# Column-tiled transposes, and bias sums moved later, at the head of a six-layer cross network on one core

## The chip, the cores and the metric

The kernel runs on one core of one Trainium2 chip. A core has TensorE (PE, matrix products; its weight loads are listed apart as PEld), VectorE (DVE), ScalarE (ACT), GpSimd (POOL), SyncE (SP, here only a queue of DMA issues) and 16 DMA engines. The metric is device time in microseconds of one execution; the median of several runs is compared. The profile is of one execution, with its own time.

## The reference, cut to what matters

```python
B, F, D, L = 4096, 26, 16, 6
Din = min(F * D, 1024)          # 416
# x0 [4096, 416], ws [6, 416, 416], bs [6, 416], all bf16
def reference(x0, ws, bs):
    x = x0
    for l in range(ws.shape[0]):
        x = x0 * (x @ ws[l] + bs[l]) + x
    return x
```

Each layer adds x0 times something to x, so x after layer l is x0 times (1 + the sum over the layers so far of x @ ws + bs). [...]

## The kernel before, in words

**Layout.** The work is done transposed, features on partitions and batch rows along the free axis. The 416 features are three chunks of 128 (c or k or m = 0, 1, 2) and a tail of 32. The 4,096 rows are four stripes of 1,024 (s), each in two halves of 512. The 32 tail features would fill only 32 partitions, so four groups of 256 rows lie side by side on 128 partitions (x0t_sb, xt_sb).

**One layer of one stripe on TensorE** (lines 318 to 431). First the *main steps* of half 0: for each of three input chunks k and three output chunks m, four matmuls of 128x32 weights side by side (`tile_mm`, L265; the tile position is a group of 32 columns of the array) over 512 rows. Then the *row matmuls* (L393, L409), which take the tail features with 32x128 weights: part 0 and part 1. Then the *tail matmuls* (L423 to L428, recorded at L265 with 256 columns), which compute the tail outputs. Then the main steps of half 1. VectorE turns each PSUM bank into the next layer's chunk (L537), ScalarE and GpSimd do the same for the tail (L595, L242, L566). Every engine follows its program in order, and semaphores (`s_...`) join them: `wait_ge(s, n)` holds the engine until s reaches n.

**The head, layer 0 of stripe 0.** Its input must first be turned. Blocks of 128x128 of x0 are loaded in natural layout into xin_sb: rows 0 to 255 (first part, h = 0, s_xin[0]), 256 to 511 (second part, h = 1), 512 to 767 (third part). The last 256 rows of the stripe come by a transposing DMA (L158), which SyncE issues once the first part has landed (L157).

- SyncE issues at L134 to L136: the biases into bsa_sb, xin_sb's first part, its third part. ScalarE issues at L137 to L139 the second part, layer 0's weights (w_sb), the tail features of the last rows (xtl_sb). VectorE clears wc_sb and sets row 0 of bsa_sb to one (L141, L142; s_zero). GpSimd makes the identity and the triangle u_sb (L211, L215; s_set) and issues small weight loads.
- TensorE runs 40 *filler* matmuls on constants (L129 to L133), then `bias_sums` (L295: 16 matmuls with 7 rows; u_sb makes running sums), one more group of four fillers (L270, L306), then the transposes of the first two parts (L308 to L316): for each of six blocks two 128x128 transposes into bf16 PSUM.
- The order of the six blocks is written out: `IN_ORDER = ((1, 0), (1, 1), (1, 2), (0, 0), (0, 1), (0, 2))`, pairs (h, c). VectorE copies blocks with c other than 1 to x0T_sb (L512, s_inD), ScalarE those with c = 1 (L562, s_inA). VectorE first copies the bias sums to cb_sb (L506, s_cb).
- Layer 0's main steps run k by k (L357): k = 0 waits for three VectorE copies (L349), k = 1 for two ScalarE copies, k = 2 for four VectorE copies. After the first of the three steps of k = 2, TensorE does the `tail_inputs` (L275: sixteen 128x32 matmuls with the identity, signal s_tp, copied by ScalarE at L576 to x0t_sb, s_te) and the `third_input` (L284: the third part, 24 matmuls with the identity into fp32 PSUM, copied at L517 and L578). Then the last two main steps.
- Row matmuls part 0 wait for x0t_sb (s_te) and five VectorE copies; part 1 for the sixth and ScalarE's third copy (L400 to L403). The tail matmuls wait for the transposing DMA (L422).

Of the kernel before, what the change touches and what calls it, by code (L numbers as in the profile page):

```python
# [11 lines left out]
def bass_standalone__dcn_v2_cross__recsys_kernel(  # L12
# [6 lines left out]
    B, D = x0.shape  # L19
# [13 lines left out]
    with ExitStack() as es:  # L33
# [22 lines left out]
        ones_sb = sb("ones_sb", [128, 256])  # L56
        bsa_sb = sb("bsa_sb", [L + 1, D])
        u_sb = sb("u_sb", [L + 1, L])
        cb_sb = sb("cb_sb", [128, NC + 1, L], FP32)
# [38 lines left out]
        IN_BANKS = ((3, 4, 6), (0, 5, 7))  # L98
        IN_ORDER = ((1, 0), (1, 1), (1, 2), (0, 0), (0, 1), (0, 2))
        THIRD = (3, 6, 7)  # L100
# [27 lines left out]

        for q in range(4 * 10):  # L129
            nc.tensor.matmul(  # L130
                ps[lane(q % 4), 7, 0:256], lhsT=CONST[:, 0:32], rhs=CONST, start=True, stop=True,
                skip_group_check=True, tile_position=(0, 32 * (q % 4)),
            )  # L133
        nc.sync.dma_start(bsa_sb[1:L + 1, :], bs[:, :]).then_inc(s_bs, 16)  # L134
        nc.sync.dma_start(xin_sb[:, 0:2, :], x0_w[:, 0, :, :]).then_inc(s_xin[0], 16)
        nc.sync.dma_start(xin_sb[:, 4:6, :], x0_w[:, 2, :, :]).then_inc(s_xin[2], 16)  # L136
        nc.scalar.dma_start(xin_sb[:, 2:4, :], x0_w[:, 1, :, :]).then_inc(s_xin[1], 16)  # L137
        nc.scalar.dma_start(w_sb[:, 0, :, :], wmain(0)).then_inc(s_w[0], 16)
        nc.scalar.dma_start(xtl_sb[:, :, :], x0_v[:, 6:JS, DF:D]).then_inc(s_xtl0, 16)  # L139
        nc.gpsimd.memset(ones_sb[:, :], 1.0).then_inc(s_ones, 1)  # L140
        nc.vector.memset(wc_sb[:, :, :], 0.0).then_inc(s_zero, 1)  # L141
        nc.vector.memset(bsa_sb[0:1, :], 1.0).then_inc(s_zero, 1)  # L142

# [59 lines left out]
        def _(pool):  # L203
            def load_wc(i, g):
# [10 lines left out]
            pool.affine_select(  # L215
                out=u_sb[:, :], in_=ones_sb[0:L + 1, 0:L], pattern=[[1, L]],
                compare_op=ALU.is_ge, fill=0.0, base=1, channel_multiplier=-1,
            ).then_inc(s_set, 1)
            for g in (0, 2):
                load_wt(pool, g, 0, 1, s_wtp)  # L220
            pool.wait_ge(s_zero, 1)
            for i in range(2):
# [3 lines left out]
            for s in range(NS):  # L226
                pool.wait_ge(s_te, s + 1)
                for l in range(L):
                    n = s * L + l + 1
                    if n == NL:  # L230
                        break
                    if n == 1:
                        pool.tensor_scalar(
                            out=cq_sb[:, 0:NC + 1], in0=cb_sb[:, :, L - 1], scalar1=-1.0, scalar2=None, op0=ALU.add
                        ).then_inc(s_cq, 1)
                        pool.wait_ge(s_cq, 1)
                        pool.tensor_tensor(
                            out=cq_sb[:, NC + 1:NC + 2], in0=cq_sb[:, NC:NC + 1], in1=cb_sb[:, NC, L - 2:L - 1], op=ALU.subtract
                        ).then_inc(s_cq, 1)
# [23 lines left out]
        def _(pe):  # L263
# [5 lines left out]

            def fill(n):  # L270
                for i in range(n):
                    for q in range(4):
                        tile_mm(ps[lane(q), 7, 0:256], CONST[:, 0:32], CONST, q, True)

# [9 lines left out]
            def third_input():  # L284
                pe.wait_ge(s_inD, 4)
                for c in range(NC):
                    for j in range(2):
                        for q in range(4):
                            f0 = c * 128 + 32 * q
                            ins = tile_mm(  # L290
                                ps[lane(q), THIRD[c], j * 128:j * 128 + 128], xin_sb[:, 4 + j, f0:f0 + 32], ident[:, :], q, True
                            )
                    ins.then_inc(s_inT, 1)

            def bias_sums():  # L295
                pe.wait_ge(s_bs, 16)
                pe.wait_ge(s_zero, 2)
                pe.wait_ge(s_set, 2)
                for c in range(NC + 1):
                    for q in range(4):  # L300
                        f0 = c * 128 + 32 * q if c < NC else DF
                        ins = tile_mm(ps[lane(q), 1, c * 8:c * 8 + L], bsa_sb[:, f0:f0 + 32], u_sb[:, :], q, True)
                ins.then_inc(s_cbp, 1)

            bias_sums()
            fill(1)  # L306
            pe.wait_ge(s_set, 1)
            for i, (h, c) in enumerate(IN_ORDER):  # L308
                if c == 0:
                    pe.wait_ge(s_xin[h], 16)  # L310
                for j in range(2 * h, 2 * h + 2):
                    ins = pe.transpose(  # L312
                        out=psT[:, IN_BANKS[h][c], (j % 2) * 128:(j % 2 + 1) * 128],
                        in_=xin_sb[:, j, c * 128:(c + 1) * 128], identity=ident[:, :],
                    )
                ins.then_inc(s_inT, 1)  # L316

            for s in range(NS):
                for l in range(L):
# [27 lines left out]
                    def before_a(k):  # L347
                        if n == 0:
                            pe.wait_ge((s_inD, s_inA, s_inD)[k], (3, 2, 4)[k])  # L349
                        else:  # L350
                            pe.wait_ge(s_xa, NC * (n - 1) + k + 1)
                            if l == 0 and k == 0:
                                pe.wait_ge(s_x0T[s], 16)

                    if n == 0:
                        pe.wait_ge(s_w[0], 16)
                        for k in range(NC):  # L357
                            before_a(k)
                            for m in range(NC):
                                if k == 0 and m == 1:  # L360
                                    pe.wait_ge(s_cb, 1)
                                if k == 2 and m == 1:
                                    pe.wait_ge(s_xin[2], 16)
# [35 lines left out]
                    for part in range(2):  # L399
                        if n == 0 and part == 1:  # L400
                            pe.wait_ge(s_inD, 6)
                            pe.wait_ge(s_inA, 3)
                            pe.wait_ge(s_wc[0], 32)  # L403
# [100 lines left out]
        def _(dve):  # L504
            dve.wait_ge(s_cbp, 1)
            dve.tensor_copy(  # L506
                out=cb_sb[:, :, :], in_=ps[:, 1, 0:8 * (NC + 1)].rearrange("p (c e) -> p c e", e=8)[:, :, 0:L],
            ).then_inc(s_cb, 1)
            for i, (h, c) in enumerate(IN_ORDER):
                if c != 1:  # L510
                    dve.wait_ge(s_inT, i + 1)
                    dve.tensor_copy(  # L512
                        out=x0T_sb[:, c, h * 256:(h + 1) * 256], in_=psT[:, IN_BANKS[h][c], 0:256]
                    ).then_inc(s_inD, 1)
            for c in (0, 2):
                dve.wait_ge(s_inT, 2 * NC + c + 1)
                dve.tensor_copy(out=x0T_sb[:, c, 512:768], in_=ps[:, THIRD[c], 0:G]).then_inc(s_inD, 1)  # L517
            dve.wait_ge(s_cb, 1)
# [37 lines left out]
        def _(act):  # L556
# [20 lines left out]
            act.wait_ge(s_inT, 2 * NC + 2)  # L577
            act.activation(out=x0T_sb[:, 1, 512:768], in_=ps[:, THIRD[1], 0:G], func=ACTF.Copy).then_inc(s_inA, 1)  # L578
            act.wait_ge(s_cb, 1)
# [79 lines left out]
```

## Time and profile before

| what | value |
|---|---|
| median of 7 runs | 128.24 us |
| all runs | 128.09, 128.13, 128.18, 128.24, 128.72, 129.0, 130.84 us |
| the profiled execution's own time | 128.19 us |
| its span in the profile | 127.0 us |
| TensorE busy | 123.4 us (97%), 2,410 matmuls |
| VectorE, ScalarE, GpSimd busy | 99.9, 67.6, 24.1 us |
| first filler starts / first transpose / first main step | 0.83 / 3.62 / 5.13 us |
| first row matmul / first tail matmul of layer 0 | 7.92 / 8.53 us |
| one layer of one stripe on TensorE | 4.87 us |
| loads of xin_sb, from issue to landing (least, median, most) | 2.5, 2.6, 3.7 us |

Times inside a profile count from the start of its span; the 1.2 us between span and time lie around it. A row of the timeline gives start, length, engine, line, operation, output and input tile, partitions x elements and the count of merged instructions; in brackets stands the idle time ahead of the first and what ended it. A matmul's length is that of one pass through the array, and matmuls overlap, so pace is read from the distance between starts. A waiting instruction is put down to the releaser that came last by the profile.

### The profile page before, as it was taken

What the parts mean: (1) busy time and instruction counts of PE and PEld (TensorE: products, weight loads), DVE (VectorE), ACT (ScalarE), POOL (GpSimd) and SP (SyncE); (2) the same over time, 40 slices, a digit from 0 to 9 for tenths busy, and PEclk for the clock granted to TensorE, in tenths of its full rate; (3) what the DMA queues carried; (4) which work ended last, traced back from release to release, by engine and by line L of the source; (5) the groups of instructions that cost most, each with busy time, mean ns of one, the idle gap of its engine ahead of it and who ended that gap; (6) DMA issues with size and microseconds to landing.
All of it is one profiled execution on the core that took longest, in us unless ns stands there. A gap on an engine that the chain in (4) does not pass through costs nothing.

```text
span 127.0 us, 5323 instructions
## 1 busy us (share of the span) xinstructions
PE 123.4 (97%) x2410; PEld 62.4 (49%) x2410; DVE 99.9 (79%) x154; ACT 67.6 (53%) x146; POOL 24.1 (19%) x44
## 2 busy tenths in 40 slices
PE   7999999999999999999999999999999999999991
PEld 5654545445445445445445445445444444454660
DVE  2449779779779779789788797797797797797973
ACT  0637357377726455575744563574762574566830
POOL 7512202202102013022022023022021021220550
PEclk9999999999999999999999999999999999999999
DMA  4952599600009879620007969970006910430006
GB/s 113 272 130 31 148 256 190 185 0 5 0 3 137 144 109 237 220 71 5 0 5 139 102 129 245 295 241 0 5 0 48 207 24 0 168 106 5 0 29 244
DMA packets 31889, 13.49 MB, mean 106 GB/s; under 512 B 24950, under 2 KB 31868, under 8 KB 31868
## 3 DMA queue, kind: packets, MB, share of 16 engines
q1 hardware_dynamic: 30476, 12.12, 45.0%
q10 hardware_dynamic: 1200, 0.99, 2.5%
q8 instruction: 19, 0.31, 1.0%
q0 software_dynamic: 192, 0.06, 0.3%
q14 instruction: 2, 0.02, 0.0%
HBM read 3.86 MB, written 3.41 MB: 57 GB/s over the span
## 4 chain that ended last, share of the span: by engine, by line
PE 97%; DVE 0%; issue 0%
PE ps L265 82%; PE ps L393 10%; PE ps L130 2%; PE ps L449 2%; PE ps L312 1%; PE ps L464 1%; DVE o_sb L550 0%; PE ps L488 0%; PE ps L409 0%; PE ps L494 0%
## 5 line engine op out<-in xcount | busy, mean ns | idle before, releaser
L537 DVE SCALAR_TENSOR_TENSOR xT_sb<-ps,cb_sb,x0T_sb 128x512 bf16<-128x512 f32 x120 | 81.0, 744 | 16.4 <-PE ps L393 16.3
L265 PE MATMUL ps<-xT_sb,w_sb 128*32 128x512 bf16 (+1 forms) x1596 | 84.2, 364 | 0.0
L265 PEld LDWEIGHTS ps<-xT_sb,w_sb 128*32 128x32 bf16 x1596 | 40.9, 97 | 37.2 <-issue 4.0
L566 ACT ACTIVATE xt_sb<-xt_sb 32x256 bf16<-32x256 bf16 x76 | 31.5, 414 | 15.7 <-POOL xt_sb L242 15.1
L595 ACT ACTIVATE t_sb<-ps,cb_sb 64x256 f32<-64x256 f32 x46 | 21.6, 469 | 31.1 <-PE ps L265 30.8
L242 POOL TENSOR_TENSOR xt_sb<-t_sb,x0t_sb 128x256 bf16<-128x256 f32 x20 | 13.5, 673 | 81.4 <-ACT t_sb L595 81.4
L265 PE MATMUL ps<-x0T_sb,w_sb 128*32 128x512 bf16 (+1 forms) x336 | 18.6, 366 | 0.0
L537 DVE SCALAR_TENSOR_TENSOR xo_sb<-ps,cb_sb,x0T_sb 128x512 bf16<-128x512 f32 x18 | 12.1, 744 | 2.5 <-PE ps L393 2.5
L265 PEld LDWEIGHTS ps<-x0T_sb,w_sb 128*32 128x32 bf16 x336 | 8.6, 97 | 7.7 <-issue 1.3
L393 PE MATMUL ps<-xt_sb,wt_sb 32*128 32x512 bf16 x76 | 11.5, 379 | 0.0
L614 ACT ACTIVATE x0t_sb<-x_sb 32x512 bf16<-32x512 bf16 x12 | 7.5, 626 | 0.3
L409 PE MATMUL ps<-xt_sb,wt_sb 32*128 32x512 bf16 x38 | 7.4, 385 | 0.0
L393 PE MATMUL ps<-xt_sb,wc_sb 32*128 32x256 bf16 x76 | 7.3, 268 | 0.0
L393 PEld LDWEIGHTS ps<-xt_sb,wt_sb 32*128 32x128 bf16 x76 | 2.2, 92 | 8.1 <-DVE xT_sb L537 8.1
L393 PEld LDWEIGHTS ps<-xt_sb,wc_sb 32*128 32x128 bf16 x76 | 3.8, 93 | 2.2
L242 POOL TENSOR_TENSOR xot_sb<-t_sb,x0t_sb 128x256 bf16<-128x256 f32 x3 | 2.0, 674 | 12.6 <-ACT t_sb L595 12.6
L550 DVE SCALAR_TENSOR_TENSOR o_sb<-ps,x0n_sb 128x416 bf16<-128x416 f32 x6 | 3.3, 585 | 1.0 <-PE ps L494 0.9
L570 ACT ACTIVATE xo_sb<-ps,cq_sb 128x512 bf16<-128x512 f32 x5 | 3.3, 686 | 1.1 <-PE ps L393 1.1
L130 PE MATMUL ps<-const-bfloat16-1.0 128*32 128x256 bf16 x40 | 2.3, 416 | 0.8 <-PEq L644 0.8
L561 ACT ACT_TABLE_LOAD x1 | 1.3, 1283 | 3.3 <-issue 3.3
L449 PE MATMUL ps<-w_sb,xT_sb 128*128 128x416 bf16 x12 | 2.8, 340 | 0.0
L265 PE MATMUL ps<-w_sb,xT_sb 128*32 128x416 bf16 x48 | 2.6, 339 | 0.0
(52 smaller groups left out, 39.9 us busy)
## 6 DMA issues: line engine op xcount, KB each, us to landing
out_dram<-o_sb SPq DMA_DIRECT2D x2, 832.0 KB, 5.3
w_sb<-in_ws_dram SPq DMA_DIRECT2D x5, 312.0 KB, 3.9
x0n_sb<-in_x_dram SPq DMA_DIRECT2D x1, 832.0 KB, 5.4
out_dram<-o_sb SPq DMA_DIRECT2D x1, 624.0 KB, 4.1
out_dram<-o_sb SPq DMA_DIRECT2D x3, 208.0 KB, 2.0
xin_sb<-in_x_dram SPq DMA_DIRECT2D x2, 208.0 KB, 3.1
out_dram<-o_sb ACTq DMA_DIRECT2D x2, 208.0 KB, 2.0
w_sb<-in_ws_dram ACTq DMA_DIRECT2D x1, 312.0 KB, 3.5
```

The costliest lines, as they stand in the source:

```text
L130: nc.tensor.matmul(ps[lane(q % 4), 7, 0:256], lhsT=CONST[:, 0:32], rhs=CONST, start=True, stop=True, skip_group_check=True, tile_position= ...
L242: pool.tensor_tensor(out=dst, in0=t32_sb[:, n % 2, :], in1=x0t_sb[:, s, 0:G], op=ALU.mult).then_inc(s_xt, 1)
L265: return pe.matmul(dst, lhsT=lhsT, rhs=rhs, start=start, stop=True, skip_group_check=True, tile_position=(0, 32 * q),)
L393: return pe.matmul(dst, lhsT=lhsT, rhs=srct[lane(g), cols], start=l == 0 and start, stop=True, skip_group_check=True, tile_position=(32 * ...
L409: pe.matmul(ps[:, NC * h + 2, :], lhsT=wt_sb[lane(g), l, 0:128], rhs=srct[lane(g), :].rearrange("p (b r) -> p b r", b=2)[:, ::-1, :], star ...
L449: pe.matmul(ps[:, NAT_BANKS[t], 0:D], lhsT=xT_sb[:, (L - 1) % 2, k, rows], rhs=w_sb[:, L - 1, k, :], start=False, stop=True, skip_group_ch ...
L537: dve.scalar_tensor_tensor(out=dst, in0=ps[:, NC * half + c, :], scalar=cb_sb[:, c, l:l + 1], in1=x0T_sb[:, c, o:o + H], op0=ALU.add, op1= ...
L550: dve.scalar_tensor_tensor(out=o_sb[:, j0 + t, :], in0=ps[:, NAT_BANKS[t], 0:D], scalar=1.0, in1=x0n_sb[:, t, :], op0=ALU.add, op1=ALU.mul ...
L566: ins = act.activation(out=buf[lane(g), G:2 * G], in_=buf[lane(g ^ 1), 0:G], func=ACTF.Copy)
L570: act.activation(out=xo_sb[:, NS - 1, c, half * H:(half + 1) * H], in_=ps[:, NC * half + c, :], func=ACTF.Identity, bias=cq_sb[:, c:c + 1] ...
L595: ins = act.activation(out=t32_sb[HALVES[h], n % 2, :], in_=tail(h), func=ACTF.Identity, bias=cb_sb[HALVES[h], NC, l:l + 1],)
L614: ins = act.activation(out=x0t_sb[lane(g), s + 1, :].rearrange("p (b n) -> p b n", b=2), in_=src[:, ::-1, :] if g % 2 else src, func=ACTF. ...
```

## The change

Fillers, transposes, bias sums, the order of the blocks and of SyncE's first loads change; what is computed does not.

- 52 fillers instead of 40; the single filler group and the `fill` helper go. `bias_sums` leaves the front.
- The transposes of all three parts become four transposes of 32 columns each side by side (`tile_tp`), in the tile shape that fillers and main steps have. The third part's now go to bf16 PSUM as well.
- Block (0,0) is turned third instead of fourth, and k = 0 waits for two VectorE copies instead of three.
- `bias_sums` stands ahead of the first main step of k = 2, followed by `tail_inputs` and `third_input`, which so stand one main step earlier. bsa_sb and u_sb get 128 partitions (zeros below the seven rows), and the sums go to bank 4 instead of bank 1. The wait for cb_sb moves from the second main step to row matmuls part 1; GpSimd gets one of its own.
- SyncE issues the biases after the two loads of xin_sb, and waits ahead of all three for VectorE's new first memset, which clears bsa_sb.

```diff
-        bsa_sb = sb("bsa_sb", [L + 1, D])
-        u_sb = sb("u_sb", [L + 1, L])
+        bsa_sb = sb("bsa_sb", [128, D])
+        u_sb = sb("u_sb", [128, L])
...
-        IN_ORDER = ((1, 0), (1, 1), (1, 2), (0, 0), (0, 1), (0, 2))
+        IN_ORDER = ((1, 0), (1, 1), (0, 0), (1, 2), (0, 1), (0, 2))
...
-        for q in range(4 * 10):
+        for q in range(4 * 13):
...
-        nc.sync.dma_start(bsa_sb[1:L + 1, :], bs[:, :]).then_inc(s_bs, 16)
+        nc.sync.wait_ge(s_zero, 1)
         nc.sync.dma_start(xin_sb[:, 0:2, :], x0_w[:, 0, :, :]).then_inc(s_xin[0], 16)
         nc.sync.dma_start(xin_sb[:, 4:6, :], x0_w[:, 2, :, :]).then_inc(s_xin[2], 16)
+        nc.sync.dma_start(bsa_sb[1:L + 1, :], bs[:, :]).then_inc(s_bs, 16)
...
+        nc.vector.memset(bsa_sb[:, :], 0.0).then_inc(s_zero, 1)
         nc.vector.memset(wc_sb[:, :, :], 0.0).then_inc(s_zero, 1)
+        nc.vector.wait_ge(s_zero, 1)
         nc.vector.memset(bsa_sb[0:1, :], 1.0).then_inc(s_zero, 1)
...
-            pool.wait_ge(s_zero, 1)
+            pool.wait_ge(s_zero, 2)
...
                     if n == 1:
+                        pool.wait_ge(s_cb, 1)
...
+            def tile_tp(dst, src, q):
+                return pe.transpose(out=dst, in_=src, identity=ident[:, :], tile_position=(0, 32 * q))
...
-                            ins = tile_mm(
-                                ps[lane(q), THIRD[c], j * 128:j * 128 + 128], xin_sb[:, 4 + j, f0:f0 + 32], ident[:, :], q, True
+                            ins = tile_tp(
+                                psT[lane(q), THIRD[c], j * 128:j * 128 + 128], xin_sb[:, 4 + j, f0:f0 + 32], q
                             )
...
             def bias_sums():
                 pe.wait_ge(s_bs, 16)
-                pe.wait_ge(s_zero, 2)
+                pe.wait_ge(s_zero, 3)
                 pe.wait_ge(s_set, 2)
+                pe.wait_ge(s_inA, 2)
...
-                        ins = tile_mm(ps[lane(q), 1, c * 8:c * 8 + L], bsa_sb[:, f0:f0 + 32], u_sb[:, :], q, True)
+                        ins = tile_mm(ps[lane(q), 4, c * 8:c * 8 + L], bsa_sb[:, f0:f0 + 32], u_sb[:, :], q, True)
...
-            bias_sums()
-            fill(1)
...
-                for j in range(2 * h, 2 * h + 2):
-                    ins = pe.transpose(
-                        out=psT[:, IN_BANKS[h][c], (j % 2) * 128:(j % 2 + 1) * 128],
-                        in_=xin_sb[:, j, c * 128:(c + 1) * 128], identity=ident[:, :],
-                    )
+                for j in range(2):
+                    for q in range(4):
+                        f0 = c * 128 + 32 * q
+                        ins = tile_tp(
+                            psT[lane(q), IN_BANKS[h][c], j * 128:j * 128 + 128], xin_sb[:, 2 * h + j, f0:f0 + 32], q
+                        )
...
-                            pe.wait_ge((s_inD, s_inA, s_inD)[k], (3, 2, 4)[k])
+                            pe.wait_ge((s_inD, s_inA, s_inD)[k], (2, 2, 4)[k])
...
-                                if k == 0 and m == 1:
-                                    pe.wait_ge(s_cb, 1)
-                                if k == 2 and m == 1:
+                                if k == 2 and m == 0:
+                                    bias_sums()
                                     pe.wait_ge(s_xin[2], 16)
                                     pe.wait_ge(s_xtl0, 16)
                                     tail_inputs()
...
                             pe.wait_ge(s_inD, 6)
+                            pe.wait_ge(s_cb, 1)
                             pe.wait_ge(s_inA, 3)
...
-            dve.wait_ge(s_cbp, 1)
-            dve.tensor_copy(
-                out=cb_sb[:, :, :], in_=ps[:, 1, 0:8 * (NC + 1)].rearrange("p (c e) -> p c e", e=8)[:, :, 0:L],
-            ).then_inc(s_cb, 1)
             for i, (h, c) in enumerate(IN_ORDER):
...
+            dve.wait_ge(s_cbp, 1)
+            dve.tensor_copy(
+                out=cb_sb[:, :, :], in_=ps[:, 4, 0:8 * (NC + 1)].rearrange("p (c e) -> p c e", e=8)[:, :, 0:L],
+            ).then_inc(s_cb, 1)
...
-                dve.tensor_copy(out=x0T_sb[:, c, 512:768], in_=ps[:, THIRD[c], 0:G]).then_inc(s_inD, 1)
+                dve.tensor_copy(out=x0T_sb[:, c, 512:768], in_=psT[:, THIRD[c], 0:G]).then_inc(s_inD, 1)
```

ScalarE's copy of the third part (L578) reads the bf16 view in the same way.

## The prediction, made before the changed kernel ran

> **What bounds the kernel now.** I read the busy times and the chain of the page first, then the first 11 us of the timeline, then one steady layer.
>
> ```profile
> span 127.0 us, 5323 instructions
> ...
> PE 123.4 (97%) x2410; PEld 62.4 (49%) x2410; DVE 99.9 (79%) x154; ACT 67.6 (53%) x146; POOL 24.1 (19%) x44
> ...
> PEclk9999999999999999999999999999999999999999
> ...
> PE 97%; DVE 0%; issue 0%
> PE ps L265 82%; PE ps L393 10%; PE ps L130 2%; PE ps L449 2%; PE ps L312 1%; PE ps L464 1%; DVE o_sb L550 0%; PE ps L488 0%; PE ps L409 0%; PE ps L494 0%
> ```
>
> TensorE is the bound: busy 123.4 of 127.0 us and 97% of the chain. From layer 1 of the first stripe on, its pieces repeat every 4.87 us with no idle. The change touches only what comes before the tail matmuls of layer 0, so its whole worth is by how much those (8.53 us) start earlier or later. Everything after them is a queue on TensorE and moves with them. These lines of the timeline (start, length, engine, line, operation, count) carry the head, first TensorE alone up to the first main step:
>
> ```profile
> 3.09 0.27 PE L265 MATMUL ps<-u_sb,bsa_sb 7*32 7x6 bf16 x16
> 3.29 0.40 PE L265 MATMUL ps<-const-bfloat16-1.0 128*32 128x256 bf16 x4
> 3.62 1.46 PE L312 MATMUL ps<-ident,xin_sb 128*128 128x128 bf16 x12
> 5.13 0.50 PE L265 MATMUL ps<-x0T_sb,w_sb 128*32 128x512 bf16 x4
> ```
>
> then the copies around the last two main steps, and after them the first row matmul and the first tail matmuls:
>
> ```profile
> 7.23 0.60 ACT L576 ACTIVATE x0t_sb<-ps 128x512 bf16<-128x512 f32 x1 [1.94 <-PE ps L265]
> ...
> 7.31 0.61 PE L265 MATMUL ps<-x0T_sb,w_sb 128*32 128x512 bf16 x8
> 7.32 0.76 DVE L517 CAST x0T_sb<-ps 128x256 bf16<-128x256 f32 x2 [1.91 <-PE ps L265]
> 7.72 0.38 ACT L578 ACTIVATE x0T_sb<-ps 128x256 bf16<-128x256 f32 x1
> ```
>
> ```profile
> 7.92 0.37 PE L393 MATMUL ps<-x0t_sb,wt_sb 32*128 32x512 bf16 x1
> ...
> 8.53 0.29 PE L265 MATMUL ps<-x0T_sb,w_sb 128*32 128x256 bf16 x4
> ```
>
> And the same passage in a steady layer:
>
> ```profile
> 11.67 1.25 PE L265 MATMUL ps<-xT_sb,w_sb 128*32 128x512 bf16 x20
> 12.86 0.38 PE L393 MATMUL ps<-xt_sb,wt_sb 32*128 32x512 bf16 x1
> ...
> 13.40 0.29 PE L265 MATMUL ps<-xT_sb,w_sb 128*32 128x256 bf16 x4
> ```
>
> The reader is to see three things. First, the pace. Forty fillers (L130, ten groups of four tiles, 256 columns) run from 0.83 for 2.33 us, one lasts 0.416 on average: (2.33-0.416)/9 = 0.213 us a group. In the steady layer five groups of 512 columns lie in 1.25 us, one lasts 0.379: (1.25-0.379)/4 = 0.217. So the head runs at half the pace. The first main step lasts 0.324 us (5.134 to 5.458 in the trace), the next 0.217: full pace began some 0.216 us into it, at 5.35. The page's row of granted clock reads 9 throughout, and the trace's only clock record starts at 5.39; before that the pace has to be read from spacing. Second, gaps where the tile shape changes: the filler of 3.29 streams until 3.50 and the 128x128 transposes start at 3.62; they stream until 4.88 and the first main step starts at 5.13, 0.14 after DVE's third copy (L512, 0.29 us each) ends at 4.99. Third, from the last main group to the tail matmuls a steady layer needs 13.40-12.54 = 0.86 us, layer 0 needs 8.53-7.53 = 1.00. The 0.14 more is waiting: x0t_sb (ACT copy to 7.83) holds the row matmuls at 7.92 instead of 7.85, and the copies of the third input (to 8.08 and 8.10) hold their second part.
>
> **The change, part by part.**
>
> Filler and bias sums at the front. Three filler groups replace the 16 bias matmuls and one filler group. The last of the ten groups starts at 2.71; it and three more at 0.213 end streaming at 3.56. xin_sb's second part has landed (issued 0.80, landed 3.31), the shape stays 128x32, so the transposes start at 3.56, not 3.62: -0.06.
>
> Transposes in column tiles. Four 32-column tiles side by side at N=128 cost (rows of L265 at 6.75 to 7.49: ten groups, one lasts 0.219) (0.74-0.22)/9 = 0.058 us a group at full pace, so 0.107 to 0.116 at half pace; one 128x128 transpose is (1.46-0.31)/11 = 0.105. Twelve groups against twelve transposes: no difference (no row streams 128 columns faster, so no gain either), if transposes on four tiles run side by side as plain matmuls do. No row shows that; the far end (one after another) is a rival below. They stream until about 4.84.
>
> Order. Block (0,0) comes third instead of fourth, and the first main step waits for two DVE copies instead of three. Third pair: streamed at 3.56+6x0.107 = 4.20, result 0.21 later (0.314-0.107), copy 0.29 from 4.44 to 4.74; plus the 0.14 seen before: 4.88. w_sb's layer 0 has landed by 4.75, xin_sb's first part (3.84) is needed at 3.99. I take 4.90 for 5.13: -0.23. Of this, half is lost because TensorE is still slow until 5.35: -0.12 of work at full pace. The ACT copies do not move (ACT's table load ends at 4.56; second copy until 5.30), but the second k is not reached before 5.79.
>
> Bias sums in the middle. They now stand ahead of the tail inputs, at full pace and on the path: 16 matmuls of 6 columns. At the front they spaced 0.027 us per four (3.137, 3.164, 3.191 in the trace), so 0.11; with both shape changes they took 0.20 (3.09 to 3.29). With bsa_sb padded to 128 rows the shape change goes. Ends 0 and 0.20; I take 0.11, nearest to the spacing. Before, they cost nothing, because TensorE was waiting for xin_sb and filler ran anyway. So they eat the 0.12 just won: the last main group stays at 7.53.
>
> Tail inputs one main step earlier. Two main steps (0.43) followed the third input, now three do. By the same sum, the last tail group starts at 6.70 (6.92 before), its signal comes at 6.98 (7.21), ACT's 0.60 us copy ends at 7.61 (7.83). The third input's copies read bf16 from PSUM: 0.29 each (the L512 rows) instead of 0.42, ready at about 7.72 on DVE and 7.89 on ACT. The waits at 7.85 and 8.07 then hold nothing: rows at 7.53+0.32 = 7.85, tail matmuls at 7.53+0.86 = **8.39 for 8.53: -0.14**. What is late next: x0T_sb by transposing DMA, landed 8.15, would hold them at about 8.24. The bias copy on DVE (0.18) moves to about 6.8, between copies; DVE is idle there (1.91 us before L517). Its reader on POOL gets a wait, which stands behind a later one (x0t_sb) and holds nothing; row part 1's new wait for it likewise.
>
> SyncE's loads. The bias load leaves the front, and a wait for DVE's first memset takes its place. The memset of 208 uint32 (rows: 480 uint32 0.46, 416 bf16 0.41; DVE starts at 0.97) lasts 0.2 to 0.41, so the first xin_sb load issues between 1.20 and 1.40, 1.25 before. Queued behind it: both xin_sb loads, the bias load, and through xin_sb's landing the x0T_sb transposes. I take 0. At the far end xin_sb lands at 4.0 and x0T_sb at 8.3, which costs at most 0.15. wc_sb's memset ends near 1.7, POOL needs it at 2.84. The bias load issues at about 2.1, behind xin_sb's third part (landed 5.35), and is needed at 6.43. Small loads of this stretch took 2.0 (bsa_sb) to 4.5 us (xtl_sb): 4.1 to 6.6. I take 5.5, since its own queue is done by then: no wait; at the far end it costs 0.2.
>
> Sum: span 127.0-0.14; the profiled execution's 128.19 becomes 128.05, and the median of 128.24 about **128.1**.
>
> [...] The row: before, twelve transposes fill 3.62 to 5.08 and full pace still came at 5.35. [...] The change adds six groups of them to the third input but also puts more filler in front, so by the row nothing changes. [...]
>
> **Rivals.**
> - The cover is gone: bias load at 6.6, bias sums 0.20, or xin_sb 0.15 later. Any of them takes back 0.1 to 0.2: 128.15 to 128.4. For: landings of 4.5 us in this stretch. Against: its place ahead of the transposing DMA on its queue.
> - More than forecast: where full pace comes before 4.9, the 0.23 counts whole and the x0T_sb landing becomes the limit: 8.24, so 127.9. Against: the record at 5.39.
> - Slower: full pace comes late, because transposes on column tiles keep TensorE less busy than full ones. Place: the main steps from 4.90 on. It decides if full pace is not there by about 6.5, over 1.3 us late (half of it is lost, 0.64 is the bound). If the slow stretch of 0.83 to 5.35 (4.5 us) started anew at the first main step, full pace would come at 9.4: (9.4-5.35)/2 = 2.0, 130.1. Against: filler runs to 3.56 without the gaps of before, and the first step starts sooner.
> - Slower too: transposes on four tiles run one after another: 36 more passes at 0.105 are 3.8 us, half of that once the pace is full, and 18 more at 0.058 are 1.0; about 132. Against: nothing but the plain matmuls' rows.
>
> **How the numbers follow.** What a measurement of this kernel can tell from no change is about 0.5%, 0.64 us: 127.60 to 128.88. Forecast 0.62, cover gone 0.17, more than forecast 0.09, a gain beyond 0.64 us 0.02 (no term reaches it), late full pace 0.07, serial tiles 0.03. Faster 0.02, same 0.88, slower 0.10. The range takes in 127.9 less 0.1, and upward all three far ends at once (128.1+0.09+0.2+0.15 = 128.54) with 0.15 for the medians (four of seven runs lie within 0.15): 127.8 to 128.7. It leaves out the two slower rivals.
>
> **What the profile after would show.** Transposes at 3.56 as 48 matmuls of 128*32; the first main group at 4.9; the bias sums near 6.4 taking 0.11; ACT's x0t_sb copy ending at 7.6; row matmuls at 7.85 and tail matmuls at 8.39; from there the same 4.87 us pieces. Wrong would be: groups of four transposes spaced over 0.12 us; a wait for the bias load ahead of the bias sums; full pace clearly after 5.4; tail matmuls held by x0T_sb.

## The result: slower by 0.6%

The changed kernel takes 129.25 us in the median of 25 runs (128.58 to 129.60); the kernel before takes 128.40 in the 60 runs beside it (127.85 to 130.84). The ratio is 1.0061, 95% interval 1.0048 to 1.0074. The forecast was 128.1 with a range up to 128.7. The comparisons leave disturbed runs out.

The profiled execution takes 129.25 us, the median itself; before it took 128.19. The page of the changed kernel answers the lines shown of before:

```profile
span 127.7 us, 5415 instructions
...
PE 123.1 (96%) x2454; PEld 62.5 (49%) x2454; DVE 99.7 (78%) x155; ACT 67.5 (53%) x146; POOL 24.0 (19%) x44
...
PE 94%; DMA 3%; issue 1%; DVE 0%; ACTq 0%
```

TensorE is busy 0.3 us less than before, and yet the span is 0.7 longer: the loss is waiting. The chain's 3% DMA, before none, is not this loss: it is the load of w_sb from 1.22 to 4.71, for which the first main step now waits the last 0.16 us. The waiting to be explained is the 0.90 us of "issue" further on. The 129.25 - 127.7 = 1.58 us around the span (by unrounded spans) were 1.23 before. So of the 1.06 us between the two profiles 0.7 lie in the span and 0.35 outside. Over all runs that list their spans the mean is 127.64 against 127.20 inside (+0.43), and 1.58 against 1.26 outside (+0.32). So the profile of before (span 127.0) was a good one of its kind, and that of the changed kernel an average one.

The timeline of the changed kernel, TensorE's rows (start, length, line, operation, then in brackets the idle time ahead):

```profile
3.56 1.03 PE L275 MATMUL ps<-ident,xin_sb 128*32 128x128 bf16 x48
4.75 1.48 PE L269 MATMUL ps<-x0T_sb,w_sb 128*32 128x512 bf16 x24 [0.16 <-DMA w_sb<-in_ws_dram]
7.13 0.27 PE L269 MATMUL ps<-u_sb,bsa_sb 128*32 128x6 bf16 x16 [0.90 <-issue]
...
7.87 0.84 PE L269 MATMUL ps<-x0T_sb,w_sb 128*32 128x512 bf16 x12
8.65 0.39 PE L394 MATMUL ps<-x0t_sb,wt_sb 32*128 32x512 bf16 x1
...
9.24 0.73 PE L269 MATMUL ps<-x0T_sb,w_sb 128*32 128x256 bf16 x16
```

The front is where the forecast put it: transposes at 3.56, the first main step at 4.75, even earlier than 4.90. Then TensorE stands for 0.90 us ahead of the bias sums, and the tail matmuls start at 9.24, 0.71 later than before. The view names only "issue" as releaser; what came last is the bias load: in the trace six of its seven completions land from 5.53 to 7.04, and the bias sums start at 7.13. So the first theory was **A: the late bias load costs it all.**

It isn't the only late load. The bias was wanted at about 6.3, but x0T_sb's transposing DMA landed at 8.87 (8.15 before), too late for the tail matmuls even if the bias sums had not waited. The view of DMAs of the changed kernel, 5 to 6 us, shows one row that the same stretch of before doesn't have (packets, MB, share of 16 engines):

```profile
q1 hardware_dynamic: 194, 0.05, 35.9%
q8 instruction: 1, 0.02, 6.0%
...
x0T_sb<-in_x_dram SPq DMA_TRANSPOSE x1, 5.0
```

It is one packet of instructions, 16 KB (16,384 bytes in the trace). The view names the queue and not the engine; that the instructions are TensorE's is inferred from its moving with the number of matmuls below. In the trace it starts at 5.08 and lasts 0.96 us, amid the 256-byte packets of the x0T_sb DMA (issue to landing 5.0 us; 4.3 before). Before, the first such packet starts at 8.58, when that DMA is done. Hence the rival, **D: more TensorE instructions in the head bring the instruction packet forward, into the landing of x0T_sb, and all loads of that stretch come late; the bias load is one of them.**

### The profile page after: what moved, and what is told of

Its sections match the earlier page's. It is cut to its first block, busy times and chain, and to the rows that moved or that the text cites. A ratio compares the mean times of both kernels' runs of the same rounds, so it can differ in the third digit from the quotient of the medians.

```text
span 127.7 us, 5415 instructions
## 1 busy us (share of the span) xinstructions
PE 123.1 (96%) x2454; PEld 62.5 (49%) x2454; DVE 99.7 (78%) x155; ACT 67.5 (53%) x146; POOL 24.0 (19%) x44
## 4 chain that ended last, share of the span: by engine, by line
PE 94%; DMA 3%; issue 1%; DVE 0%; ACTq 0%
PE ps L269 81%; PE ps L394 10%; DMA w_sb<-in_ws_dram 3%; PE ps L451 2%; PE ps L466 1%; DVE o_sb L552 0%; PE ps L490 0%; ACTq L138 0%; PE ps L275 0%; PE ps L411 0%; PE ps L496 0%
## 5 line engine op out<-in xcount | busy, mean ns | idle before, releaser
L130 PE MATMUL ps<-const-bfloat16-1.0 128*32 128x256 bf16 x52 | 3.0, 419 | 0.8 <-PEq L646 0.8
L130 PEld LDWEIGHTS ps<-const-bfloat16-1.0 128*32 128x32 bf16 x52 | 2.2, 144 | 1.1 <-issue 0.8
```

The lines of the kernel that those rows point to most:

```text
L130: nc.tensor.matmul(ps[lane(q % 4), 7, 0:256], lhsT=CONST[:, 0:32], rhs=CONST, start=True, stop=True, skip_group_check=True, tile_position= ...
```

## The experiments

The table puts all 18 kernels together. "Matmuls" are those that the trace lists ahead of the first row matmul; the next three columns are of the one profiled execution (us; the packet is the first of 16 KB on queue q8). "Span" is the mean span less that of the kernel before, run beside it (good to about 0.25), "outside" the median of time less span; before has 1.24 to 1.27 there each time.

| run | matmuls | packet starts | x0T_sb landed | tail matmuls | span | outside | ratio to before, 95% interval |
|---|---|---|---|---|---|---|---|
| before / e4 | 148 | 8.58 / 7.45 | 8.15 / 8.05 | 8.53 / 8.41 | 0 | 1.26 | 1 |
| after | 192 | 5.08 | 8.87 | 9.24 | +0.43 | 1.59 | 1.0061 (1.0048 to 1.0074) |
| e1 | 192 | 5.30 | 8.68 | 8.72 | +0.86 | 1.57 | 1.0091 (1.0062 to 1.0121) |
| e2 | 192 | 5.12 | 8.90 | 10.02 | +0.56 | 1.60 | 1.0062 (1.0031 to 1.0093) |
| e3 | 184 | 6.71 | 8.77 | 8.81 | +0.43 | 1.27 | 1.0032 (1.0007 to 1.0057) |
| e5 | 188 | 6.70 | 8.01 | 8.81 | +0.33 | 1.29 | 1.0023 (1.0001 to 1.0046) |
| e6 | 147 | 7.56 | 7.99 | 8.70 | +0.26 | 1.49 | 1.0035 (1.0009 to 1.0061) |
| e7 | 113 | 8.67 | 8.19 | 9.21 | -0.05 | 1.33 | 1.0004 (0.9979 to 1.0029) |
| e8 | 147 | 8.45 | 8.41 | 9.11 | +0.24 | 1.49 | 1.0034 (1.0012 to 1.0056) |
| e9 | 116 | 8.36 | 7.94 | 8.84 | +0.24 | 1.26 | 1.0033 (1.0005 to 1.0061) |
| e10 | 160 | 7.35 | 8.11 | 8.22 | -0.11 | 1.25 | 0.9994 (0.9970 to 1.0019) |
| e11 | 148 | 8.01 | 7.74 | 8.80 | -0.06 | 1.27 | 0.9993 (0.9960 to 1.0025) |
| e12 | 180 | 6.61 | 9.78 | 9.82 | +0.13 | 1.51 | 1.0019 (0.9996 to 1.0042) |
| e13 | 192 | 5.32 | 9.05 | 9.10 | +0.40 | 1.60 | 1.0063 (1.0040 to 1.0086) |
| e14 | 148 | 8.03 | 8.41 | 11.45 | +2.26 | 1.25 | 1.0175 (1.0141 to 1.0210) |
| e15 | 184 | 5.48 | 8.89 | 8.93 | +0.55 | 1.25 | 1.0038 (1.0008 to 1.0068) |
| e16 | 156 | 8.95 | 8.11 | 8.37 | +0.17 | 1.56 | 1.0035 (1.0011 to 1.0059) |
| e17 | 156 | 8.34 | 8.27 | 9.32 | +0.34 | 1.55 | 1.0045 (1.0022 to 1.0069) |
| e18 | 148 | - | - | - | -0.23 | 1.24 | 0.9981 (0.9954 to 1.0007) |

(e18's profile is of an execution of 130.37 us, far from its median of 128.45, and has no place in these columns.)

Two things help to read the table. Span less the start of the tail matmuls is 118.42 to 118.44 us in 18 of the 19 profiles (118.75 in e16), so "Span" tells how much later the tail matmuls start on average, and one profile is one draw. And where no load is late, the tail column follows the moment at which TensorE reached full pace in that execution: 3.95 in e10 (tail 8.22), 5.00 in e4 (8.41), 5.39 in before (8.53), 6.1 in e11 and e9 (8.80 and 8.84).

### The bias load itself: e1, e2

e1 issues the bias load second instead of third:

```diff
         nc.sync.dma_start(xin_sb[:, 0:2, :], x0_w[:, 0, :, :]).then_inc(s_xin[0], 16)
+        nc.sync.dma_start(bsa_sb[1:L + 1, :], bs[:, :]).then_inc(s_bs, 16)
         nc.sync.dma_start(xin_sb[:, 4:6, :], x0_w[:, 2, :, :]).then_inc(s_xin[2], 16)
-        nc.sync.dma_start(bsa_sb[1:L + 1, :], bs[:, :]).then_inc(s_bs, 16)
```

> The changed kernel with one line moved: SyncE issues the bias load between the first and the third part of xin_sb instead of after both. Theory A (the bias load lands late, at 7.04 us, and holds TensorE for 0.87 us ahead of the bias sums): its landing moves to about 4, TensorE does not stop at the second k's end, first tail matmul at 8.4 to 9.0 instead of 9.24, time 128.4 to 129.0 instead of 129.25. Rival B (the transposing DMA of x0T_sb, which landed at 8.87 us instead of 8.15, would hold the tail matmuls anyway): they start at 8.96, time 128.95, and TensorE now waits for x0T_sb. Rival C (the loss lies in the column tiles or the bias sums themselves): no change, 129.25.

e2 calls `bias_sums()` behind the last main step of half 0 instead of ahead of the tail inputs, and VectorE's copy of them comes last.

> The changed kernel with the bias load left last, but the bias sums moved behind the last main step of half 0, and VectorE's copy of them behind the third input's copies. Theory A: the load has landed when TensorE gets there (about 7.1 us), the 0.87 us stop goes, first tail matmul at 8.4 to 9.0, time 128.4 to 129.0. Rival B: the same 8.96 and 128.95 as with the load moved. Rival C: 129.25.

Both took away the wait for the bias, and neither won anything: 129.58 and 129.25 us. In e1 the load landed at 4.64 and the bias sums ran without a wait. TensorE's rows of e1:

```profile
6.22 0.27 PE L269 MATMUL ps<-u_sb,bsa_sb 128*32 128x6 bf16 x16
6.32 0.24 PE L269 MATMUL ps<-ident,xin_sb 128*32 128x128 bf16 x3
...
7.64 0.38 PE L394 MATMUL ps<-x0t_sb,wt_sb 32*128 32x512 bf16 x1
...
8.18 0.37 PE L394 MATMUL ps<-x0t_sb,wt_sb 32*128 32x512 bf16 x1
...
8.72 0.51 PE L269 MATMUL ps<-x0T_sb,w_sb 128*32 128x256 bf16 x12
```

Up to the first row matmul (7.64, forecast 7.85) e1 is better than the forecast. Then part 1 waits until 8.18 (wc_sb landed at 8.04) and the tail matmuls until 8.72 (x0T_sb at 8.68). In e2 it is xtl_sb that comes late, at 7.69:

```profile
7.83 0.24 PE L269 MATMUL ps<-ident,xin_sb 128*32 128x128 bf16 x3 [1.39 <-DMA xtl_sb<-in_x_dram]
```

Each time another load of the same stretch takes the place of the wait removed. Theory A as the whole cause falls: the widest gap in the profile is only the first of several.

### Fewer or more instructions in the head: e3 to e8

e3 takes tiles and order alone: `tile_tp` for the first two parts, `IN_ORDER`, and the wait `(2, 2, 4)`; third part, bias sums and loads as before.

> The kernel before with one part of the change alone: the first two parts turned in four 32-column tiles side by side, block (0,0) third and the first main step waiting for two VectorE copies. Bias load first and bias sums at the front as before, third input as before. The prediction's terms: first main step at about 4.9 instead of 5.13, first tail matmul 0.1 to 0.25 us earlier than in the kernel before, ratio 0.998 to 0.999. Rival C (column tiles cost time): groups of four transposes more than 0.12 us apart at half pace, first main step not earlier, ratio 1.000 or above.

e4 is the kernel before once more, for a second profile.

> The kernel before, profiled once more, to see when TensorE reaches full pace. [...] In the changed kernel it came at about 3.8 us.

e5 is before with twice the fillers at half the length, e7 before with few and large ones, e6 the changed kernel with few and large ones, e8 is e6 with e1's order of loads (`WIDE` is a constant of 512 columns):

```diff
 # e5, in the kernel before
-        for q in range(4 * 10):
+        for q in range(4 * 20):
...
-                ps[lane(q % 4), 7, 0:256], lhsT=CONST[:, 0:32], rhs=CONST, start=True, stop=True,
+                ps[lane(q % 4), 7, 0:128], lhsT=CONST[:, 0:32], rhs=CONST[:, 0:128], start=True, stop=True,
 # e7 in the kernel before: range(5); e6 and e8 in the changed one: range(6) and one more of 256 columns
+        for q in range(5):
...
+                ps[:, 7, :], lhsT=WIDE[:, 0:128], rhs=WIDE, start=True, stop=True, skip_group_check=True,
```

> The kernel before with one edit: the 40 fillers of 256 columns become 80 of 128 columns, so the front lasts as long with 80 more TensorE instructions (40 matmuls and their weight loads). Theory D (the first 16 KB packet of the instruction queue comes when TensorE has used up its first instructions; more instructions bring it from 7.4 to 8.6 us forward to 5 to 6, among the loads of the head, and what those loads feed comes late): packet at 5 to 6.5 us, x0T_sb lands at 8.6 to 8.9 instead of 8.05 to 8.15, first tail matmul at 8.7 to 9.0 instead of 8.41 to 8.53, time 128.8 to 129.2 instead of 128.4. Rival E (the loss belongs to column-tiled transposes or to the bias sums): nothing of these is in this kernel, 128.4.

> The changed kernel with one edit: the 52 fillers on column tiles become six of the full array with 512 columns and one with 256, the same length at the front with 90 fewer TensorE instructions. Bias load still last. Theory D: the instruction queue's packet comes after 7.5 us, x0T_sb lands at 8.1 to 8.3, the bias load lands earlier than 7.04, first tail matmul at 8.3 to 8.6 instead of 9.24, time 128.2 to 128.6 instead of 129.25. Rival E: fillers are not concerned, 129.25.

> The kernel before with its 40 fillers made five of the full array with 512 columns: 70 fewer TensorE instructions at the same length of the front. Theory D: the packet moves from 7.4 to 8.6 us to 9 or later, the loads of the head land as before or a little earlier, first tail matmul at 8.3 to 8.5, time 128.1 to 128.4. Rival E: 128.4. It also shows whether the spread of the kernel before (127.85 to 129.1) comes from this packet: by theory D it narrows.

> The changed kernel with the few fillers of the full array and the bias load between the first and third part of xin_sb. Theory D with theory A in second place: bias landed by 4.7 us, no stop ahead of the bias sums, x0T_sb at 8.1 to 8.3, first tail matmul 8.3 to 8.4, time 128.0 to 128.3. Rival E: 129.2 to 129.6 as with the bias load moved alone.

The packet follows the number of matmuls both ways. e5 has none of the change, only 40 more fillers, and the packet comes at 6.70 instead of 7.45 to 8.58. e6 has all of the change and 45 matmuls fewer; the packet comes at 7.56 instead of 5.08, x0T_sb lands at 7.99, the bias at 6.13. Nothing stands ahead of its bias sums any more:

```profile
6.67 0.26 PE L272 MATMUL ps<-u_sb,bsa_sb 128*32 128x6 bf16 x16
6.77 0.23 PE L272 MATMUL ps<-ident,xin_sb 128*32 128x128 bf16 x3
...
8.70 0.51 PE L272 MATMUL ps<-x0T_sb,w_sb 128*32 128x256 bf16 x12
```

e6 takes 128.77 us in the median, 0.48 less than the changed kernel; by the ratios it is 0.26% less, and the two intervals still touch. It stays behind before by 0.35%. e8, with the early bias load as well, was expected at 128.0 to 128.3 and takes 128.83, no better than e6. e5 was a miss for theory D in part: the packet came earlier, but x0T_sb landed at 8.01 and not at 8.6 to 8.9. As e5 is the only kernel with many matmuls and no tiled transposes, it isn't shown that the count alone, whatever the matmuls, brings the late loads. e7, where the packet is late, still runs from 128.06 to 129.15, which speaks against the packet as the source of the spread of before. e3 was a miss for both theories: tiles and order alone cost 0.32%, with the bias load early and, at a packet of 6.71, no hold of the loads but one late completion of x0T_sb (8.77, the others by 7.99).

### What lies outside the span, and the order alone: e9 to e12

The idea was that the count of fillers sets the time outside. e9 is before with 8 full-array fillers of 320 columns, e10 before with 52 fillers of 196 columns, e12 the changed kernel with 40 of 332 columns. e11 is before with the new `IN_ORDER` and `(2, 2, 4)` alone.

> The kernel before, with its 40 column-tile fillers (two records each in the trace) replaced by 8 full-array fillers of 320 columns, as long in all. Theory that the time outside the span depends on how many instructions TensorE has ahead of the block (1.23 us with 40 or 80 fillers, 1.5 with 5 or 52): either a matter of the count (then about 1.5, median 128.4) or of where the block falls in its instruction stream (16 filler instructions, a multiple of 16 as 80 and 160 are: then 1.23, median 128.05). Rival, that the time outside doesn't follow the fillers at all: any value. The 16 KB packet of TensorE's instruction queue is expected at 8 us or later (8.67 with 5 fillers), and the landing of x0T_sb at about 8.2.

> The kernel before with 52 column-tile fillers of 196 columns instead of 40 of 256: as many filler instructions as the changed kernel, no longer in time, nothing else of the change. If the number of fillers alone sets the 0.35 us that the changed kernel loses outside its span: time less span about 1.58, and a median of 128.7 to 128.8. If it also moves the 16 KB instruction packet into the landing of x0T_sb: the packet at about 5 to 6 us and another 0.3 to 0.5. If neither: 128.4, time less span 1.23, packet at 7.4 to 8.6.

> The order part alone: block (0,0) transposed third and the first main step waiting for two VectorE copies, full-array transposes, bias sums and loads as before. The prediction's step: first main step at 4.9 to 5.0 instead of 5.13, which is worth 0.12 us on the slow clock if the full pace comes at 5.35, all of 0.2 if it comes before 4.9. Span 0.05 to 0.2 shorter, time less span 1.23 as before; median 128.2 to 128.4. Rival, that the landing of x0T_sb (about 8.1) takes the gain: 128.4.

> The changed kernel with 40 column-tile fillers of 332 columns instead of 52 of 256: as long in all, 24 instructions fewer on TensorE. Theory that the instruction count matters: time less span falls from 1.58 to 1.23, the 16 KB packet of the instruction queue moves from 5.1 to later, x0T_sb lands before 8.4 and the median is 128.5 to 128.9. Rival, that the bias load's late landing is all of it: packet may move, yet the bias load still lands near 7 and the median stays at 129.25.

The idea fell: e10 has the changed kernel's 52 fillers and 1.25 us outside, e12 has before's 40 and 1.51. (e9 shows 1.2 to 1.3 in seven of its twelve runs and 1.5 or more in five; e7 wavers likewise.) The order alone is worth nothing that can be measured. e12's profile, one of its slowest runs, had w_sb land late, at 5.60, and the packet at 6.61 still met loads that were under way. Its runs lie between before and after: the interval takes in before, but doesn't reach the changed kernel's (1.0042 against 1.0048). So 12 fillers fewer, at the same length of the front, go with some 0.4% less time.

### Loads, waits and tiles one by one: e13 to e16

e13 is the changed kernel with before's loads: the bias load first, no wait on SyncE, 7-row bsa_sb and u_sb. e16 is e13 with the full-array transposes of before for the first two parts (12 matmuls for 48). e15 is before with tiles in the old order. e14 is before with SyncE's wait for the 128-row memset ahead of its three loads.

> The changed kernel with SyncE's loads, the memsets and the 7-row tiles of the bias as before (bias load first, landing near 2.8 us); tiles, order and the bias sums ahead of the tail inputs as in the change. Theory that SyncE's wait and the late bias load cost both the time outside the span and some 0.2 to 0.4 inside: time less span 1.25 for 1.58, median 128.4 to 128.7. Theory that the 16 KB instruction packet amid the x0T_sb transposes is what counts: the packet stays near 5.1, x0T_sb lands at 8.6 to 8.9, tail matmuls at 8.7 to 8.9. If the prediction's steps held but for the loads: tail matmuls at 8.4, median 128.1.

> The kernel before with one thing of the change: the 128-row bias tile zeroed by VectorE first, and SyncE waiting for that ahead of its first load (the bias load, still first; the xin_sb loads behind it go out 0.35 us later each). If SyncE's wait is what lengthens the time outside the span: 1.5 to 1.6 for 1.25 there, and with 0.1 to 0.2 inside for the later xin_sb a median of 128.8 to 129.0. If not: 1.25 outside, 128.5 to 128.7.

> The kernel before with the first two inputs transposed in 128x32 column tiles (48 matmuls for 12), order, loads and bias sums as before. If the 72 more instructions on TensorE are what made tiles with the new order cost 0.3% (while the order alone cost nothing): 16 KB packet at 7 us or earlier, median 128.7 to 128.9. If the tiles cost nothing, as the prediction had it: 128.4, no less.

> As e13_loads_as_before, but with the full-array transposes of before for the first two inputs: order, bias sums ahead of the tail inputs, third input in tiles, longer filler, loads as before. If the tiles cost 0.3 to 0.4 us: that much below e13_loads_as_before, 128.1 to 128.3, the best of all. If they don't: equal to it.

e13 has its bias at 2.19 us, as early as could be, and takes 129.11 us: 1.0063, the same as the changed kernel. With e1 and e2 this speaks against the late bias load as the cause, but e13 doesn't measure it alone: its bias sums have 7 rows again and take 0.19 us longer in the trace (see below), which may hide as much. e13 against e16 is tiles alone: 129.11 and 128.81, 0.23 of it in the span, 36 matmuls and a packet at 5.32 or 8.95. e16 was expected to be the best of all, at 128.1 to 128.3; 0.35% stay with its tiles gone. e15 has tiles alone on before's side: packet at 5.48 and +0.38%. What the packet does shows in the view of DMAs for 6.5 to 7.0 us, of e15, then of e16:

```profile
DMA  0020202000110102001100200101011020011010
...
DMA packets 18, 0.00 MB, mean 9 GB/s; under 512 B 18, under 2 KB 18, under 8 KB 18
```

```profile
DMA  9995644335224351993433495338753919959899
...
DMA packets 186, 0.08 MB, mean 151 GB/s; under 512 B 114, under 2 KB 186, under 8 KB 186
```

The first row is the busy share of the 16 DMA engines in slices. With the packet at 5.48 the DMAs all but stand still in this stretch: 18 packets in 0.5 us, one each 28 ns, against 186. In the trace of e15, 21 of the transposing packets that started between 6.08 and 6.48 all end within 40 ns of 7.26. In each of the six profiles with such a hold (after, e1, e2, e13, e15, and e12 with other packets) it ends 0.80 to 0.90 us after the instruction packet does. In five of them it also begins only after the packet's end, at 6.45 to 6.60.

e15 and e10 (before with tiles, and before with 52 shorter fillers) show what a hold costs at an equal pace: both reached full pace at nearly the same moment (3.93 and 3.95 by the clock records of their traces), e15 with the packet at 5.48, e10 at 7.35. TensorE's rows of e15, then of e10:

```profile
6.96 0.62 PE L265 MATMUL ps<-x0T_sb,w_sb 128*32 128x512 bf16 x8
...
7.90 0.37 PE L397 MATMUL ps<-x0t_sb,wt_sb 32*128 32x512 bf16 x1 [0.32 <-DVE x0T_sb L521]
...
8.93 0.73 PE L265 MATMUL ps<-x0T_sb,w_sb 128*32 128x256 bf16 x16 [0.19 <-DMA x0T_sb<-in_x_dram]
```

```profile
7.00 0.62 PE L266 MATMUL ps<-x0T_sb,w_sb 128*32 128x512 bf16 x8
...
7.62 0.37 PE L394 MATMUL ps<-x0t_sb,wt_sb 32*128 32x512 bf16 x1
...
8.22 1.37 PE L266 MATMUL ps<-x0T_sb,w_sb 128*32 128x256 bf16 x28
```

e15 comes to its last two main steps 0.04 us earlier and to its tail matmuls 0.71 later; x0T_sb landed at 8.89 and 8.11.

e14 cost far more than expected, by another route. Its timeline:

```profile
3.58 0.82 PE L315 MATMUL ps<-ident,xin_sb 128*128 128x128 bf16 x6
5.45 0.82 PE L315 MATMUL ps<-ident,xin_sb 128*128 128x128 bf16 x6 [1.04 <-DMA xin_sb<-in_x_dram]
6.32 3.18 PE L268 MATMUL ps<-x0T_sb,w_sb 128*32 128x512 bf16 x28
```

xin_sb's first part was issued at 1.62 instead of 1.25, 0.40 behind ScalarE's load of w_sb (1.22) where it was 0.03 behind, and landed at 5.40 instead of 3.84. That w_sb's load is what kept it is argued and not shown. TensorE stood 1.04 us and then stayed at half pace: main groups 0.43 apart up to 9.3, full pace only near 10. The time outside was 1.25: SyncE's wait isn't what lengthens it.

### The last two suspects: e17, e18

Both stand on e11's order. e17 moves the bias sums and has 52 fillers (e16 with the third part as before); e18 has the third part as PE transposes into bf16.

> On the order of e11_order_only: the bias sums ahead of the tail inputs and the filler of the change (52) instead of sums and one filler group at the front; loads, full-array transposes and the third input (plain matmuls, f32 copies) as before. If the moved sums and filler are what lengthens the time outside the span: 1.5 to 1.6, median 128.7 to 128.8. If not: 1.25, 128.4.

> On the order of e11_order_only: the third input as PE transposes into bf16 PSUM (copies of 0.29 us for 0.42), all else as before. If that is what lengthens the time outside the span: 1.5 to 1.6 and a median near 128.7. If not, and the prediction's step holds (row matmuls' second part no longer held by the copies, up to 0.1 us, once x0T_sb has landed): 1.25 outside, 128.3 to 128.4.

e17 has 1.55 us outside, e18 1.24. So the 0.3 us outside come with the bias sums moved out of the front (and the filler up to 3.56 that takes their place; the two were not parted). All nine kernels that have it (after, e1, e2, e6, e8, e12, e13, e16, e17) show 1.49 to 1.60; e7 and e9 reach 1.5 in part of their runs without it. e17 is also the strongest sign that the instruction packet isn't all: with full-array transposes and the packet at 8.34, when x0T_sb has landed, it loses 0.45%. e18 is the lowest of all, but 0.9981 with an interval to 1.0007 doesn't show it faster than before; no version was found that beats both kernels.

## Why the prediction was wrong, step by step

**Right.** That everything after the tail matmuls moves with them (118.4 us in all profiles but one). The front (3.56). The tiles: groups of four transposes 0.107 us apart, 0.056 at full pace, so they do run side by side. The bias sums: 0.10 from their start to the next group in e1, e6 and e12 (0.11 forecast), 0.18 behind the stand in the changed kernel itself; with 7 rows, in e13, 0.11 of gap ahead and 0.18, so the padding to 128 rows saves up to 0.19. The third input's copies on VectorE: 0.29 each, as forecast (the row's 0.52 takes in two that overlap). ScalarE's copy, at 8.28 after x0t_sb, still takes 0.38; the forecast 0.29 was VectorE's figure, and ScalarE's bf16 copies before (L561) already took 0.38.

```profile
7.79 0.60 ACT L578 ACTIVATE x0t_sb<-ps 128x512 bf16<-128x512 f32 x1 [2.60 <-PE ps L269]
7.88 0.52 DVE L519 COPY x0T_sb<-ps 128x256 bf16<-128x256 bf16 x2 [0.23 <-PE ps L275]
```

With them the tail matmuls follow the last main group by 9.24 - 8.30 = 0.94 us in the changed kernel (1.00 before, 0.86 forecast). SyncE's wait on the memset did not move xin_sb, as forecast (3.31 and 3.81).

The 0.61% fall into two parts of roughly the same size. Kernels that keep all or most of the change with fewer instructions and a later packet (e6, e8, e12, e16) still lose 0.19% to 0.35%; the rest goes away with the instructions. So two steps failed.

**Wrong, the step that shows first: no term for the instructions themselves.** The prediction counted each added matmul by its time on TensorE and put the tiles at "no difference". It costed nothing for the packets that bring them. Tiles alone measure +0.38% (e15), +0.32% with the order (e3), and 0.30 us in the median between e13 and e16. Of the 19 profiles in the table, the 11 with up to 160 matmuls in the head have the packet at 7.35 us or later, the 8 with 180 or more at 5.08 to 6.71. So "x0T_sb by transposing DMA, landed 8.15" was taken as a constant and was 8.87.

By the traces of before and after these packets have 16,384 bytes each, on queue q8, 19 in each execution. In the six profiles with a hold the loads stood still until 0.80 to 0.90 us after the end of the first one. Nothing shows TensorE itself waiting for instructions in the changed kernel: its stand ended 0.09 us after the last completion of the bias load. That the loads stood because they share the DMA engines with the packet is argued, not shown.

**Wrong, the other half: moved bias sums and longer filler put at nothing in sum.** The forecast took 0.11 for the sums, won back by the order, and 0.06 gained by the filler. The runs show +0.23 to +0.29 us outside the span in all kernels with the moved sums and a late packet (e6, e8, e16, e17), and +0.17 to +0.34 inside it. Inside, the sums' own price covers much of this: 0.29 with 7 rows in e13, and in e16 and e17, which have 7 rows too, 0.17 and 0.34 were lost; with 128 rows it is 0.10, and e6 and e8 lost 0.26 and 0.24.

**Wrong: "I take 5.5, since its own queue is done by then: no wait".** The bias load landed at 7.04, above the far end of 6.6. Its last completions land at 6.90 to 7.04, right after the hold ends near 6.89; without the hold (e6) it is 6.13. So the cover gone, the rival priced at 0.2, did happen and showed as 0.90 in the profile; yet with that wait gone (e1, e2, e13) the loss stayed, since other late loads took its place.

**Wrong: the time outside the span carried over unchanged.** It grew by 0.32 us, over a third of the loss, and no view of before showed that.

**Wrong: full pace at 5.35 as a fixed point.** In the changed kernel transposes go from 0.107 to 0.056 us a group at 3.9; in the other profiles but e14 full pace came anywhere from 3.7 to 6.6, and at 5.39 and 5.00 in the two of the kernel before. With one profile of each kernel a relation to the edits can't be told. The 0.12 that the order was to win depends on it in each run; e11 measures no gain, but its interval takes in 0.1% too.

**What stays open.** Why the packet falls where it does within each group (e3 and e15 have equally many matmuls, 6.71 and 5.48). It isn't a fixed place in the stream: at its start TensorE had executed from 188 (e14) to 376 (e16) matmuls and weight loads. Why a packet at 6.70 (e3, e5) brings no hold, and why e5, whose one profile shows no late load and only a late full pace (6.0), still has +0.33. Why the DMAs hold: one packet each 28 ns looks like one engine that works off its own backlog while the rest wait for it, but the trace doesn't name engines, so that is argued and not shown. What the 0.3 us outside the span consist of. And what of the +0.17 to +0.34 inside, with moved sums and a late packet, is more than the sums' own time: it is near the limit of what 12 runs can tell.

## What to carry to other kernels

Count the instructions that a change adds ahead of a critical load, not only their time: 128x32 tiles do the work of one full-array transpose in four instructions (here 48 for 12), and with 36 more of them an instruction packet came into the middle of the loads (at 5.32 us in e13, at 8.95 in e16). Count as well what leaves its free place: work that ran while TensorE waited anyway has its full price once it stands on the path (here the bias sums: 0.29 us with 7 rows in e13, 0.10 with 128 in e6). When a profile shows one wide wait, ask which other waits would hold at nearly the same time before you price its removal; here taking it away (e1, e2, e13) won nothing. And compare time less span as well as the span: an edit can cost there too (here 0.32 us).

## What the runs showed of the hardware

- A 16 KB instruction packet took 0.88 to 1.66 us on its queue (the 38 of before and after). Where it started at 5.08 to 5.48, amid a transposing DMA (after, e1, e2, e13, e15), DMA traffic fell to some 9 GB/s from 6.45 to 6.60 on, up to 0.80 to 0.90 us after the packet's end. Packets at 6.70 (e3, e5) and 7.35 (e10) also ran amid that DMA, and no such stretch followed.
- Full pace came in the midst of transposes in after, e1, e7, e10, e12, e13 and e15, at 3.7 to 4.4 us, behind fillers; in after the groups of four went from 0.107 to 0.056 us there.
- The only late full pace of the table (e14, near 10 us) followed a stand of 1.04 us ahead of it; in e18's profile TensorE stood 0.88 us for w_sb ahead of the first main step, and half pace lasted until 8.9. The changed kernel's stand of 0.90 us came after full pace, and the next groups were at 0.056 us again.
- A load issued 0.36 us later landed 1.55 later (e14, xin_sb behind w_sb's 312 KB).
